# Norm 1's scale and shift moved to ScalarE on transposed rows, modulation sums in column groups, GpSimd in source order, attention's list shifted

## The chip, the cores and the metric

One core of a Trainium2 chip runs the whole kernel. The metric is the device time of one execution in microseconds (us). PE is TensorE's matrix multiply and PEld its weight load, DVE is VectorE, ACT is ScalarE, POOL is GpSimd, and SP is SyncE, which here only issues transfers.

## The reference, cut to what matters

A transformer block for one sequence of 2048 rows and 576 channels. Six modulation vectors come from a condition vector. The first layer norm is scaled and shifted by two of them and feeds a sliding-window attention with 32 heads of 18 channels; the second half (a shifted token mixer and an MLP with 4608 hidden channels) is not touched by the change.

```python
mod = (silu(c) @ w_mod).reshape(1, 6, 1, 576)
sa, ca, ga, sb, cb, gb = mod[:, 0], ..., mod[:, 5]
h = layernorm(x) * (1 + ca) + sa                 # norm 1
q, k, v = split(h @ wqkv)                        # 3 x 32 heads x 18
p = softmax(where(0 <= i - j < 256, q k^T * 18**-0.5, -1e9))
x = x + ga * ((p v) @ wo)
h = layernorm(x) * (1 + cb) + sb
x = x + gb * B(h)                                # mixer and MLP
```

## The kernel before

Matrices are split into a rounded part and the rest of it (F32R), so that one product is the sum of three: high times high, high times low, low times high. The work of attention is in `phase_a`. It makes a list of timed steps (`ev`) and plays it in order of time; the times are in units of 12.5 us, only order the steps, and are no measurement. PE runs its instructions in that order (`manual_schedule` names PE). The other engines' streams, and SP's transfers, are ordered by a scheduler. Each engine works its stream off strictly in order.

**Start.** `cond` loads the condition vector `c` one element to a partition and makes silu of it. `mod_load(v)` loads the part of `w_mod` for vector v (v = 1 is the scale `ca`, v = 0 the shift `sa`) as one tile `wmL`, in one large transfer and one for the last 64 rows. `mod_mm` multiplies a 128-column copy of silu (`silub`) with it, in two halves of 288 columns and five chunks of rows each, so that each sum `pm` stands on all 128 partitions; `mod_ev` evicts it into a row tile `mod`.

**Norm 1** runs for 16 tiles t of 128 rows: `load` (x to a row buffer, tag "r", 5 buffers), `stat` (DVE's bn_stats, POOL's rs), `norm` (`modulate`, L95 to L106: DVE L99 and L101, for t of 2 and more DVE L99 and POOL L103 and L104, on whole rows) and `tr` (`split9`: five PE transposes L68 and L72 into two PSUM tiles `pa` and `pb` of tag "tr" with two buffers, ACT casts L69 and L73 to the high part of `hT`, DVE subtractions L70 and L74 for the low part).

**Projections.** `vproj(t, z)` makes a `pv` (14 matmuls of 288 columns, L316) for half z of the value heads, `qproj(m, g)` a `pq` (14 matmuls of 512 columns, L330) for 128 channels m of queries and keys and 4 tiles g of rows. Order in PE's stream: for g = 0 to 3 four `pv` of z = 0 and the two `pq` of m = 0 and 4, with the transposes of the next group between them; then 16 `pv` of z = 1; then the other `pq`. The weights `Wv` and `Wq` are loaded by SP, cast by ACT and completed by a subtraction on POOL (L280, L294). A `pq` is cast by ACT (L332) and subtracted by DVE (L333) into `hl`, which SP stores to the DRAM tensors `qkh` and `qkl` (L335).

**Attention** works on 32 units of four heads by 512 rows. `ualloc` takes four tiles `U` (three of them in the buffers of `hT`, the fourth in that of `Wq`), and sets them to 0 (DVE, L344) and 1 (POOL, L345). `uload` fills a `U` with 12 loads from `qkh` and `qkl` (SP, L359). `s2` makes the scores `sc` of 16 blocks (PE L385) whose maxima DVE reduces (L392), turns the maxima (`mT`, L406) and writes them into U by a DMA (`ms`, L410); `s3` makes the exponents (`X` on PE L435 and L436, `P` on ACT L442) and the products with V (`av`, L457, four heads on four groups of 32 partitions). The list of attention begins at `shift = t_end + u0`, where `t_end` is the time behind the last `pq`.

The other four modulation vectors are summed up on POOL in `modvec` (chunks L187 to L190), and PE adds over the partitions (L197) at fixed places in attention.

Of the kernel before, what the change touches and what calls it, by code (L numbers as in the profile page):

```python
# [50 lines left out]
class Kern:  # L51
# [75 lines left out]
    def phase_a(self):  # L127
# [10 lines left out]
        with ExitStack() as st:  # L138
# [25 lines left out]
            def cond():  # L164
                ct = sm.tile([P, KC + 1], F32, name="ct", bufs=1)
                nc.vector.memset(ct, 0.0)
                with nc.allow_non_contiguous_dma("condition vector to partitions"):
                    nc.sync.dma_start(ct[:, 0:KC], self.c[0, 0:KC * P].rearrange("(k p) -> p k", p=P))
                    nc.sync.dma_start(ct[:TAIL, KC:KC + 1], self.c[0, KC * P:].rearrange("(k p) -> p k", p=TAIL))
                nc.scalar.activation(silu, ct, AF.Exp, scale=-1.0)  # L170
                nc.vector.tensor_scalar(silu, silu, 1.0, None, op0=ALU.add)
                nc.vector.reciprocal(silu, silu)
                nc.vector.tensor_tensor(out=silu, in0=silu, in1=ct, op=ALU.mult)
# [49 lines left out]

            def mod_bc():
                fm["s"] = pp.tile([P, KC + 1, P], F32, tag="P", name="silub", bufs=self.b_p)
                nc.vector.tensor_copy(fm["s"], silu.unsqueeze(2).to_broadcast([P, KC + 1, P]))

            def mod_mm(v, hf):
                def f():
                    cs = slice(hf * 288, (hf + 1) * 288)  # L230
                    pm = self.ps.tile([P, 288], F32, tag="sc", name=f"pm{v}{hf}", bufs=self.b_sc)
                    for k in range(KC + 1):
                        kk = P if k < KC else TAIL
                        nc.tensor.matmul(pm, fm["s"][:kk, k, :], fm[v][:kk, k, cs], start=(k == 0), stop=(k == KC))
# [3 lines left out]
            def mod_ev(v, hf):
                def f():
                    cs = slice(hf * 288, (hf + 1) * 288)  # L240
                    if hf == 0:
                        mod2[v] = rp.tile([P, D], F32, tag="cs", name=f"mod{v}", bufs=4)
                    nc.scalar.activation(mod2[v][:, cs], fm[v, hf], AF.Copy, bias=1.0 if v == 1 else 0.0)
                return f
# [24 lines left out]

            def vload(z, k):  # L270
                def f():
                    raw = rp.tile([P, 288], F32, tag="wraw", name=f"rwv{z}_{k}", bufs=2)
# [6 lines left out]
                    nc.scalar.copy(w[:, 0, :], raw)
                    nc.gpsimd.tensor_tensor(out=w[:, 1, :], in0=raw, in1=w[:, 0, :].bitcast(F32), op=ALU.subtract)  # L280
# [40 lines left out]
            def qproj(m, g):  # L321
                def f():
# [11 lines left out]
                    for n, dst in enumerate((qkh, qkl)):  # L334
                        nc.sync.dma_start(dst[m * P:(m + 1) * P, g * 512:(g + 1) * 512], hl[:, n, :].bitcast(F32))  # L335
                return f

            def ualloc(n):
                def f():
# [4 lines left out]
                    nc.vector.memset(q.bitcast(F32), 0.0)  # L344
# [728 lines left out]
```

## Time and profile before

| | us |
|---|---|
| median of 3 runs | 1852.71 (1848.93 to 1860.01) |
| profiled execution | 1854.05 |
| its span in the trace | 1851.9 |
| PE busy | 1770.5 (96%) |
| DVE, ACT, POOL busy | 1005.2, 583.4, 399.9 |
| granted TensorE clock, mean | 0.979 of full |

The span runs from the first to the last instruction. A busy PE is no PE at its peak: under a lower granted clock the same matmul is busy for longer, so the clock column is read beside the busy one. In a timeline, the first number is the start, the second the busy time, and brackets hold the idle time of the engine ahead of the group and what ended it.

### The profile page before, as it was taken

To read this page: it belongs to the slowest core of one execution; us is meant where nothing else is said; L and a number is where in the kernel's file an instruction comes from. 1 tells how busy PE (TensorE), PEld (TensorE's weight loads), DVE (VectorE), ACT (ScalarE), POOL (GpSimd) and SP (SyncE) were. 2 spreads that over 40 slices of the span, in tenths; PEclk is the share of its full clock that TensorE was granted. 3 is DMA by queue.
4 is the path that set the end of the run, shared out by engine and by line. 5 is a ranking of instruction groups with operands and counts; after the bars stand their busy time and mean duration, and the time that the engine had idled before them with its cause. 6 is when DMAs were issued, how large, how long until landed. Compare 5 with 4: busy or idle time off the path is not lost.

```text
span 1851.9 us, 30277 instructions
## 1 busy us (share of the span) xinstructions
PE 1770.5 (96%) x11696; PEld 1517.7 (82%) x11696; DVE 1005.2 (54%) x2683; ACT 583.4 (32%) x1212; POOL 399.9 (22%) x389
## 2 busy tenths in 40 slices
PE   6889979999998988899999999999999999999999
PEld 4788856667675776899989999999999999999998
DVE  5601267777775787887744444444444344444433
ACT  2222226656565444434321112111211121112111
POOL 7771100000002011111133323332232111111100
PEclk8999979999998999999999999999999999999999
DMA  6454443333334455642211111111110000000002
GB/s 183 118 145 138 168 129 90 91 96 96 94 97 127 146 181 181 224 154 84 85 53 53 53 34 47 53 53 41 34 47 20 28 28 28 28 28 28 1 1 103
DMA packets 98502, 156.88 MB, mean 85 GB/s; under 512 B 11828, under 2 KB 41268, under 8 KB 98360
## 3 DMA queue, kind: packets, MB, share of 16 engines
q1 hardware_dynamic: 98360, 154.97, 27.3%
q8 instruction: 92, 1.51, 0.3%
q14 instruction: 50, 0.41, 0.1%
HBM read 107.06 MB, written 47.20 MB: 83 GB/s over the span
## 4 chain that ended last, share of the span: by engine, by line
PE 55%; DVE 2%; POOL 1%; issue 0%; ACT 0%; DVEq 0%; ACTq 0%; POOLq 0%
PE p L1001 25%; PE p L972 21%; PE pg L813 2%; PE w L866 2%; PE p L974 2%; PE p L973 2%; DVE x L867 0%; DVE xr L99 0%; PE po L638 0%; DVE G L831 0%; POOL CW L956 0%; DVE LNT L70 0%; DVE G L818 0%; DVE CW L951 0%; DVE xm L740 0%
## 5 line engine op out<-in xcount | busy, mean ns | idle before, releaser
L1001 PEld LDWEIGHTS p<-CW,Gc 128*128 128x128 f32 x3456 | 474.7, 188 | 16.2 <-DVE Gc L983 3.6
L1001 PE MATMUL p<-CW,Gc 128*128 128x288 f32 x3456 | 483.1, 295 | 3.4 <-DVE Gc L983 3.4
L972 PE MATMUL p<-LNT,CW 128*128 128x512 f32 x1728 | 419.3, 391 | 0.0
L972 PEld LDWEIGHTS p<-LNT,CW 128*128 128x128 f32 x1728 | 316.6, 188 | 58.8
L1005 DVE TENSOR_TENSOR acc<-p,acc 128x288 f32<-128x288 f32 x340 | 153.6, 455 | 317.0 <-PE p L1001 313.6
L392 DVE CUSTOM_DVE_ANT_0 sc<-sc,mask 128x384 f32<-128x384 f32 (+2 forms) x512 | 264.4, 553 | 105.8 <-PE sc L385 99.7
L980 ACT ACTIVATE gfc<-p 128x512 f32<-128x512 f32 x144 | 86.2, 599 | 735.7 <-PE p L974 735.7
L442 ACT ACTIVATE P<-X 128x384 f32<-128x384 f32 x480 | 228.7, 490 | 151.7 <-PE X L436 144.7
L385 PE MATMUL sc<-U 126*128 126x384 f32 (+2 forms) x512 | 204.6, 420 | 14.2 <-DMA U<-qkh 7.5
L435 PE MATMUL X<-U 128*128 128x384 f32 (+2 forms) x704 | 194.3, 331 | 10.6 <-ACT P L442 6.8
L435 PEld LDWEIGHTS X<-U 128*128 128x128 f32 x704 | 124.8, 194 | 61.8 <-ACT P L442 31.5
L1005 DVE TENSOR_TENSOR accw<-p,accw 128x288 f32<-128x288 f32 x204 | 90.0, 453 | 130.4 <-PE p L1001 129.1
L436 PE MATMUL X<-maskb,identb 128*128 128x256 bf16 x480 | 138.1, 288 | 0.0
L983 DVE TENSOR_TENSOR Gc<-gfc,Gc 128x512 fp32r<-128x512 f32 x144 | 129.0, 896 | 5.3 <-ACT Gc L982 0.7
L385 PEld LDWEIGHTS sc<-U 126*128 126x128 f32 x512 | 103.1, 207 | 22.3 <-issue 9.0
L330 PE MATMUL pq<-hT,Wq 128*128 128x512 f32 x504 | 120.3, 399 | 0.0
L330 PEld LDWEIGHTS pq<-hT,Wq 128*128 128x128 f32 x504 | 95.2, 190 | 22.4
L952 POOL TENSOR_TENSOR CW<-r,CW 128x1024 fp32r<-128x1024 f32 x17 | 41.2, 2426 | 281.6 <-DVE CW L950 281.6
L457 PE MATMUL av<-P,V 128*32 128x256 f32 (+2 forms) x1472 | 95.0, 392 | 0.0
L982 ACT CAST Gc<-gfc 128x512 fp32r<-128x512 f32 x144 | 89.4, 621 | 4.6
L956 POOL TENSOR_TENSOR CW<-r,CW 128x1152 fp32r<-128x1152 f32 x17 | 46.5, 2733 | 158.4 <-DVE CW L955 158.4
L517 POOL TENSOR_TENSOR wor<-wor,ga 128x576 f32<-128x576 f32 x5 | 7.0, 1401 | 337.5 <-DMA wor<-in_A_wo_dram 337.5
(1076 smaller groups left out, 2027.3 us busy)
## 6 DMA issues: line engine op xcount, KB each, us to landing
U<-qkh SPq DMA_DIRECT2D x160, 72.0 KB
U<-qkh SPq DMA_DIRECT2D x96, 108.0 KB
r<-in_B_w_dram SPq DMA_DIRECT2D x18, 576.0 KB
qkh<-hl SPq DMA_DIRECT2D x36, 256.0 KB
qkl<-hl SPq DMA_DIRECT2D x36, 256.0 KB
r<-in_B_w_dram SPq DMA_DIRECT2D x18, 512.0 KB
U<-qkl SPq DMA_DIRECT2D x80, 72.0 KB
U<-qkl SPq DMA_DIRECT2D x48, 108.0 KB
```

Source lines behind the costliest of these rows:

```text
L330: nc.tensor.matmul(pq, a, b, start=(n == 0), stop=(n == len(pl) - 1))
L385: nc.tensor.matmul(sc[:, lo:], QZ[:KR, q, i * P:(i + 1) * P], KZ[:KR, j, i * P + lo:(i + 3) * P], start=True, stop=True)
L392: nc.vector.tensor_tensor_reduce(out=sc[:, lo:], in0=sc[:, lo:], in1=mask[:, lo:], scale=1.0, scalar=-3e38, op0=ALU.add, op1=ALU.max, accu ...
L435: nc.tensor.matmul(X[:, x0:x0 + nb, :].rearrange("p a b -> p (a b)"), KZ[:, j, kb * P:(kb + 1) * P], QZ[:, q, qb * P:(qb + nb) * P], start ...
L436: nc.tensor.matmul(X[:, 0::2, :], self.identb, mk, start=False, stop=True)
L442: nc.scalar.activation(Pb[b][:, q, :], Xb[b, q].rearrange("p a b -> p (a b)"), AF.Exp, scale=SCALE)
L457: nc.tensor.matmul(abox[0][32 * q:32 * q + 32, q0:q0 + w], V[4 * g + kb][:, hv:hv + 32], Pb[b][:, q, p0:p0 + w], start=(first and n == 0), ...
L972: nc.tensor.matmul(pg, W3[:, ws, fs], L[:, xs, :], start=(i == 0), stop=False)
L982: nc.scalar.copy(Gh, gf)
L983: nc.vector.tensor_tensor(out=Gl, in0=gf, in1=Gh.bitcast(F32), op=ALU.subtract)
L1001: nc.tensor.matmul(po, a, w, start=(i == 0), stop=(i == len(seq) - 1))
L1005: nc.vector.tensor_tensor(out=acc[t][:, cs], in0=po, in1=acc[t][:, cs], op=ALU.add)
```

## The change

- `cond` loads `c` as five rows, and PE turns it onto the partitions (`pc`).
- `mod_load` and `mod_mm` go by row chunks k: two loads of 128 rows, then four matmuls with only 32 columns of silu, one for each quarter q (shift or scale, columns 0 to 255 or 256 to 575), that write four groups of 32 partitions of one PSUM tile `pm`. `mod_ev` evicts the four, and `mod_tr` turns them so that scale and shift stand per channel on partitions (`modT`).
- `norm` is only subtract and multiply on DVE (one `tensor_scalar`). Scale and shift are applied behind the transposes by ACT, five ACTIVATE Identity of 128 columns whose scale and bias are columns of `modT`: four write back into the row tile x, one into PSUM. ACT then casts; the low part of 4 x 128 columns is subtracted by POOL instead of DVE.
- `Wv` is loaded by one large transfer a half (`vraw`); for z = 0 DVE subtracts instead of POOL. The four `pq` of m = 5 stand ahead of the 16 `pv` of z = 1, and the last three m (7, 3, 8) go by groups, so that hT0 is last read nine `pq` ahead of the end (six before).
- The `hl` stores are issued by ACT instead of SP. The `U` zeros are set by POOL instead of DVE.
- POOL runs in the order of the list too; `u0` goes from 0.3 to -1.55, `u_ld` from 0.45 to 0.5, and the times of the start are a new table.

```diff
 def mod_mm(k):
+    for q in range(4):
+        v, cs = q // 2, halves[q % 2]
+        nc.tensor.matmul(fm["p"][32 * q:32 * q + 32, 0:cs.stop - cs.start], fm["s"][:kk, k, :], fm[v][:kk, k, cs], start=(k == 0), stop=(k == KC))
...
 def norm():
-    self.modulate(x, x, box[0], box[1], mod2[1], mod2[0], self.m_eng[t])
+    nc.vector.tensor_scalar(x, x, box[0], box[1], op0=ALU.subtract, op1=ALU.mult)
 def tr():
...
+    for k in range(KC):
+        nc.scalar.activation(h[:, k, :], pa[:, k, :], AF.Identity, bias=mod_col(0, k, r), scale=mod_col(1, k, r))
+    nc.scalar.activation(pb, pb, AF.Identity, bias=mod_col(0, KC, r), scale=mod_col(1, KC, r))
+    nc.scalar.copy(L[:, 0:KC, cs], h)
+    nc.scalar.copy(L[:TAIL, 2 * KC, cs], pb)
+    nc.gpsimd.tensor_tensor(out=L[:, KC:2 * KC, cs], in0=h, in1=L[:, 0:KC, cs].bitcast(F32), op=ALU.subtract)
+    nc.vector.tensor_tensor(out=L[TAIL:, 2 * KC, cs], in0=pb, in1=L[:TAIL, 2 * KC, cs].bitcast(F32), op=ALU.subtract)
...
-    nc.gpsimd.tensor_tensor(out=w[:, 1, :], in0=raw, in1=w[:, 0, :].bitcast(F32), op=ALU.subtract)
+    (nc.gpsimd if z else nc.vector).tensor_tensor(out=w[:, 1, :], in0=raw, in1=w[:, 0, :].bitcast(F32), op=ALU.subtract)
...
-    nc.sync.dma_start(dst[m * P:(m + 1) * P, g * 512:(g + 1) * 512], hl[:, n, :].bitcast(F32))
+    nc.scalar.dma_start(dst[m * P:(m + 1) * P, g * 512:(g + 1) * 512], hl[:, n, :].bitcast(F32))
...
-    nc.vector.memset(q.bitcast(F32), 0.0)
+    nc.gpsimd.memset(q.bitcast(F32), 0.0)
...
-    u0, u_ld = 0.3, 0.45
+    u0, u_ld = -1.55, 0.5
-    with self.tc.manual_schedule(engines={mybir.EngineType.PE}):
+    with self.tc.manual_schedule(engines={mybir.EngineType.PE, mybir.EngineType.Pool}):
```

PE's stream at the start before, from the modulation sums to the first row tile (`x_249` is tile 0):

```order
L234 MATMUL pm_219<-wmL_211,silub 128x288 x5
L234 MATMUL pm_225<-wmL_211,silub 128x288 x5
L234 MATMUL pm_233<-wmL_214,silub 128x288 x5
L234 MATMUL pm_240<-wmL_214,silub 128x288 x5
L68 MATMUL hT0pa<-ident,x_249 128x128 x4
L72 MATMUL hT0pb<-ident,x_249 64x128
```

The same place now; the last of the five chunks and the turns behind it (`pc_320` becomes `modT`):

```order
L242 MATMUL pm<-wmL_255,modx 32x256
L242 MATMUL pm<-wmL_255,modx 32x320
L242 MATMUL pm<-wmL_253,modx 32x256
L242 MATMUL pm<-wmL_253,modx 32x320
L254 MATMUL pc_320<-ident,modx 128x128 x2
L255 MATMUL pc_320<-ident,modx 64x128
L285 MATMUL hT0pa<-ident,x_215 128x128 x4
L287 MATMUL hT0pb<-ident,x_215 64x128
```

The sums moved from 20 matmuls on 128 partitions to 20 on 32 partitions each, three transposes came in behind them, and tile 0's transposes no longer read rows that hold scale and shift.

POOL's stream before, around the subtractions for `Wv` of z = 1 (`Wv_1` to `Wv_3` of that half; `wm` are chunks of `modvec`):

```order
L189 TENSOR_SCALAR wm_3_3986<-wm_3_3986,silu 128x576
L190 TENSOR_TENSOR wm_0_3767<-wm_0_3767,wm_3_3986 128x576
L280 TENSOR_TENSOR Wv_1_1128<-rwv_1_1127,Wv_1_1128 128x288
L280 TENSOR_TENSOR Wv_2_1133<-rwv_2_1132,Wv_2_1133 128x288
L189 TENSOR_SCALAR wm_4_4065<-wm_4_4065,silu 64x576
L190 TENSOR_TENSOR wm_0_3767<-wm_0_3767,wm_4_4065 64x576
L187 TENSOR_SCALAR wm_0_4244<-wm_0_4244,silu 128x576
L189 TENSOR_SCALAR wm_1_4315<-wm_1_4315,silu 128x576
L190 TENSOR_TENSOR wm_0_4244<-wm_0_4244,wm_1_4315 128x576
L280 TENSOR_TENSOR Wv_3_1138<-rwv_3_1137,Wv_3_1138 128x288
```

And now, from the last tile's subtraction on (`x_793` is tile 15):

```order
L296 TENSOR_TENSOR hT_942<-x_793,hT_942 128x4x128
L334 TENSOR_TENSOR Wq<-rwq_1126,Wq 128x640
L320 TENSOR_TENSOR Wv_0_1148<-rwv_1073,Wv_0_1148 128x288
L320 TENSOR_TENSOR Wv_1_1151<-rwv_1073,Wv_1_1151 128x288
L320 TENSOR_TENSOR Wv_2_1154<-rwv_1073,Wv_2_1154 128x288
L320 TENSOR_TENSOR Wv_3_1157<-rwv_1073,Wv_3_1157 128x288
L320 TENSOR_TENSOR Wv_4_1160<-rwt_1075,Wv_4_1160 128x288
L334 TENSOR_TENSOR Wq<-rwq_1475,Wq 128x640
```

The chunks of `modvec` are gone from between them; they now stand behind the eight settings of `U`.

PE's stream before, from the last `pq` to attention:

```order
L330 MATMUL pq_2_1929<-hT_706,Wq 128x512 x14
L330 MATMUL pq_2_1952<-hT_706,Wq 128x512 x14
L330 MATMUL pq_3_1972<-hT_903,Wq 128x512 x14
L330 MATMUL pq_3_1995<-hT_903,Wq 128x512 x14
L385 MATMUL sc_0_0_0_0_2031<-U_1906 128x128
L385 MATMUL sc_0_0_0_1_2033<-U_1906 128x128
L385 MATMUL sc_0_0_0_2_2036<-U_1906 128x128
L385 MATMUL sc_0_0_0_3_2039<-U_1906 128x128
```

And now, from the last `pq` that reads hT0 (`hT_363`) on:

```order
L370 MATMUL pq_0_1855<-hT_363,Wq 128x512 x14
L370 MATMUL pq_1_1875<-hT_514,Wq 128x512 x14
L370 MATMUL pq_1_1898<-hT_514,Wq 128x512 x14
L370 MATMUL pq_1_1930<-hT_514,Wq 128x512 x14
L370 MATMUL pq_2_1950<-hT_733,Wq 128x512 x14
L425 MATMUL sc_0_0_0_0_1974<-U_1895 128x128
L425 MATMUL sc_0_0_0_1_1976<-U_1895 128x128
L425 MATMUL sc_0_0_0_2_1979<-U_1895 128x128
L425 MATMUL sc_0_0_0_3_1982<-U_1895 128x128
L425 MATMUL sc_0_0_1_0_1985<-U_1895 128x256
L370 MATMUL pq_2_1988<-hT_733,Wq 128x512 x14
L425 MATMUL sc_0_0_1_1_2008<-U_1895 128x256
```

The first 25 scores moved in ahead of, among and behind the last five `pq`: five, then four behind each `pq`. From the first `X` on PE's stream is the same as before.

More of the change, by code (lines that the diff above doesn't have):

```diff
@@ L164, in cond @@
             def cond():
[L165 to L173, printed above, removed]
+                fm["x"] = pp.tile([P, 12 * P], F32, tag="P", name="modx", bufs=self.b_p)
+                cr = fm["x"][0:KC + 1, 9 * P:10 * P]
+                sr = fm["x"][0:KC + 1, 10 * P:11 * P]
+                nc.vector.memset(cr, 0.0)
+                nc.sync.dma_start(cr[0:KC, :], self.c[0:1, 0:KC * P].rearrange("o (k p) -> (o k) p", p=P))
+                nc.sync.dma_start(cr[KC:KC + 1, 0:TAIL], self.c[0:1, KC * P:])
+                nc.scalar.activation(sr, cr, AF.Exp, scale=-1.0)
+                nc.vector.tensor_scalar(sr, sr, 1.0, None, op0=ALU.add)
+                nc.vector.reciprocal(sr, sr)
+                nc.vector.tensor_tensor(out=sr, in0=sr, in1=cr, op=ALU.mult)
+                pc = self.ps.tile([P, KC + 1], F32, tag="tr", name="pc", bufs=self.b_tr)
+                nc.tensor.transpose(pc, sr, self.ident[0:KC + 1, 0:KC + 1])
+                nc.vector.tensor_copy(silu, pc)
             def modvec(v):
@@ L238, in mod_ev @@
[L238 to L244, printed above, removed]
+                fm["s"] = fm["x"][:, 4 * P:4 * P + 32 * (KC + 1)].rearrange("p (k n) -> p k n", n=32)
+                nc.vector.memset(fm["x"][:, 256:320], 0.0)
@@ new lines, in mod_ev, with mod_tr @@
+            def mod_ev():
+                fm["r"] = fm["x"][:, 0:320]
+                for q in range(4):
+                    n = halves[q % 2].stop - halves[q % 2].start
+                    nc.scalar.activation(fm["r"][32 * q:32 * q + 32, 0:n], fm["p"][32 * q:32 * q + 32, 0:n], AF.Copy, bias=float(q // 2))
+            def mod_tr():
+                pc = self.ps.tile([P, 3, P], F32, tag="tr", name="pc2", bufs=self.b_tr)
+                for j in range(2):
+                    nc.tensor.transpose(pc[:, j, :], fm["r"][:, j * P:(j + 1) * P], self.ident)
+                nc.tensor.transpose(pc[:TAIL, 2, :], fm["r"][:, 2 * P:2 * P + TAIL], self.ident)
+                v4 = pc.rearrange("p j (q n) -> p q j n", n=32)
+                nc.vector.tensor_copy(modT[:, :, 0:2], v4[:, :, 0:2, 0])
+                nc.vector.tensor_copy(modT[:TAIL, :, 2:3], v4[:TAIL, :, 2:3, 0])
@@ L246, in ln, with mod_col @@
+            def mod_col(v, k, rows):
+                q, j = (2 * v, k) if k < 2 else (2 * v + 1, k - 2)
+                return modT[rows, q, j:j + 1]
             def ln(t):
@@ L565, in phase_a @@
                 else:
-                    first.setdefault(("q", a), T)
                     ev.append((T, qproj(a, b)))
```

101 lines of the change are left out of this document (55 added, 46 removed).

## The prediction

> **What bounds the kernel now.** I read the page's busy shares first, then a table of stages, then who PE waited for, then PE's own order of events.
>
> ```profile
> PE 1770.5 (96%) x11696; PEld 1517.7 (82%) x11696; DVE 1005.2 (54%) x2683; ACT 583.4 (32%) x1212; POOL 399.9 (22%) x389
> ```
>
> PE is the bound, and PE's stream is fixed. So the change can save PE's idle time, and the time that PE runs at a low clock; the rest stays. Where these lie the table of stages shows (start and end, length, then busy us and instructions of PE, PEld, DVE, ACT, POOL, then granted clock, DMA share, GB/s):
>
> ```profile
> 0.00:25.54 25.54, 16.91 (x57) 8.92 (x57) 11.98 (x29) 5.43 (x12) 15.40 (x64) 1.00 0.70 214
> 25.54:36.01 10.47, 4.90 (x20) 3.57 (x21) 7.35 (x11) 4.18 (x10) 10.47 (x9) 0.50 0.30 81
> 36.01:58.55 22.54, 19.50 (x106) 17.30 (x105) 15.80 (x31) 5.42 (x14) 18.53 (x23) 0.86 0.49 145
> 58.55:76.41 17.86, 16.32 (x108) 14.72 (x105) 12.47 (x25) 5.54 (x15) 13.26 (x16) 1.00 0.45 125
> 76.41:94.34 17.93, 16.39 (x107) 14.79 (x105) 6.85 (x15) 5.53 (x15) 11.49 (x14) 1.00 0.44 127
> 94.34:108.47 14.13, 14.13 (x88) 12.86 (x86) 1.57 (x3) 3.40 (x9) 12.61 (x13) 1.00 0.60 165
> 108.47:147.67 39.20, 32.66 (x225) 31.86 (x224) 1.88 (x6) 9.29 (x23) 23.58 (x23) 0.91 0.42 119
> 147.67:239.36 91.69, 91.69 (x394) 73.57 (x392) 23.54 (x30) 18.77 (x32) 12.60 (x9) 1.00 0.47 167
> 239.36:259.06 19.70, 10.93 (x30) 7.18 (x30) 13.12 (x54) 1.16 (x2) 1.38 (x1) 0.61 0.37 110
> 259.06:265.16 6.10, 6.10 (x38) 5.09 (x38) 4.18 (x15) 2.46 (x5) 0.00 (x0) 0.56 0.52 161
> 300.00:900.00 600.00, 565.68 (x4650) 447.78 (x4650) 455.23 (x1546) 318.87 (x730) 52.08 (x97) 0.98 0.42 127
> 900.00:1851.90 951.90, 943.06 (x5640) 858.83 (x5637) 426.39 (x831) 184.29 (x310) 228.48 (x126) 1.00 0.13 40
> ```
>
> The stages are: modulation sums; first transposes; the four groups of `pv` and `pq`; the `pv` of z = 1; the other `pq`; the scores ahead of the first X; attention's first pieces. From 265 on nothing in PE's order changes. What PE waited for in the first 300 us (engine, line, releaser: total, times, longest):
>
> ```profile
> PE sc L385 <- DMA U<-qkh: 6.5, 1, 6.5
> PE pv L316 <- POOL Wv L280: 5.2, 2, 3.3
> PE hT0pa L68 <- DVE x L101: 3.9, 1, 3.9
> PE hT3pa L68 <- POOL Wv L280: 3.0, 1, 3.0
> PE hT6pa L68 <- POOL x L103: 2.9, 1, 2.9
> ```
>
> Each wait stands where the change reaches. PE's events (start, busy, group, idle before):
>
> ```profile
> 10.26 11.34 PE L234 MATMUL pm<-wmL,silub 128*128 128x288 f32 x40 [3.71 <-DVE silub L226]
> 25.54 1.12 PE L68 MATMUL hT0pa<-ident,x 128*128 128x128 f32 x4 [3.94 <-DVE x L101]
> 36.01 7.18 PE L316 MATMUL pv<-Wv,hT 128*128 128x288 f32 x42
> 94.34 7.75 PE L316 MATMUL pv<-Wv,hT 128*128 128x288 f32 x56
> 101.93 6.70 PE L330 MATMUL pq<-hT,Wq 128*128 128x512 f32 x28
> 247.19 7.93 PE L385 MATMUL sc<-U 126*128 126x128 f32 x18 [0.85 <-DMA U<-qkl]
> 264.37 0.86 PE L457 MATMUL av<-P,V 128*32 128x256 f32 x16
> 265.78 0.60 PE L385 MATMUL sc<-U 126*128 126x384 f32 x2
> ```
>
> By starts, a `pv` takes (101.93 - 94.34) / 4 = 1.90 us and a `pq` (108.47 - 101.93) / 2 = 3.27 at full clock. Useful work begins at 36.0.
>
> **A. The start: first `pv` from 36.0 to about 25.7, gain 10.3.** Transfers come first (a window of the queue's full load; the first row tile; the condition vector, whose landing lets ACT's table load begin):
>
> ```profile
> 2.00:16.00 14.00, 10.29 (x36) 5.13 (x34) 4.83 (x17) 2.34 (x5) 4.70 (x42) 1.00 1.00 324
> 12.75 0.46 DVE L85 BATCH_NORM_STATS2 a0st<-x 128x6 f32<-128x288 f32 x1 [2.55 <-DMA x<-in_A_x_dram]
> 7.21 1.28 ACT L170 ACT_TABLE_LOAD   x1 [7.21 <-DMA ct<-in_c_dram]
> ```
>
> The first row tile lands at 12.7 behind 2.95 MB (both `wmL` and itself), that is 9.1 us at 324 GB/s from 2.0 on, and 1.6 more. Now two row tiles, `c` and the ten chunks are first, 3.24 MB: the last chunk lands at 2.0 + 10.0 + 1.6 = 13.6, and `Wv` (0.74 MB) at 15.9. `c` no longer stands behind a large transfer; silu is ready by 8, hidden by the chunks. The sums: before, a record of 288 columns takes 11.34 / 40 = 0.283 us, two records a matmul. In `av`, eight matmuls on four groups of 32 partitions (16 records, 256 and 128 columns) would take 3.0 us at that rate and take 0.8, so the four groups run beside each other. The four of the last chunk then take about 0.6. Evictions, turns and copies follow; ACT's prices come from these rows:
>
> ```profile
> 26.69 0.59 ACT L69 CAST hT<-hT0pa 128x512 fp32r<-128x512 f32 x1 [0.48 <-PE hT0pa L68]
> 27.17 0.43 ACT L279 CAST Wv<-rwv 128x288 fp32r<-128x288 f32 x1
> 27.50 0.26 ACT L73 CAST hT<-hT0pb 64x128 fp32r<-64x128 f32 x1
> 27.66 0.43 ACT L279 CAST Wv<-rwv 128x288 fp32r<-128x288 f32 x1
> ```
>
> POOL's price for a row operation on two tensors (mean 1453 ns for 576 columns), and SP's for issuing a store of `hl`:
>
> ```profile
> L104 POOL TENSOR_TENSOR x<-x,mod 128x576 f32<-128x576 f32 x14 | 20.3, 1453 | 0.8
> 207.34 0.32 SPq L335 DMA_DIRECT2D qkh<-hl  x1
> ```
>
> On ACT, from start to start, 512 columns take 0.48, 288 take 0.33, 128 take 0.16. Four evictions 1.3, three transposes 0.9 (the row of 25.54 has four in 1.12), two small DVE copies 0.4, handing over 0.3: `modT` at 17.1. On ACT five casts of `Wv` stand ahead of tile 0, from 15.9 to 17.6. The new ACTIVATE with scale and bias from partitions is in no row: between 0.16 and 0.48, and I take 0.33, since columns of `modT` have to be fetched. Tile 0 frees its PSUM tile at 17.6 + 4 x 0.33 = 18.9. Since `tr` has two buffers, each next tile costs transposes 1.1 (low clock, as in the second stage), 1.3 on ACT and 0.2 of handing over, 2.6 in all; tile 3's transposes end at 18.9 + 2 x 2.6 + 1.1 + 0.4 = 25.6. POOL's subtraction of a tile (512 of L104's 576 columns, 1.3) lies beside it. Ends: 36.0 - 23 = 13 with 0.16 an ACTIVATE; 4 with 0.48 and sums that run one behind another (20 x 0.57 from 8 on, 19.4 instead of 14.2).
>
> ScalarE: Activation LUTs, What ACT_TABLE_LOAD costs, in the Trainium skill, gives an ACTIVATE 186 ns and 0.833 ns a column, 93 ns more for each operand that is a column of partitions, and an overlap of 93 ns. The 288-column row fits (0.43). For the new ones it gives 0.39 a start; the first `pv` would then come at about 26.5, and ACT would have 15.5 us of work in a group instead of 14.3.
>
> **B. The groups: gain 4.7.** Without its idle 1.54 a group takes 16.3 (the row of 58.55). The first took 22.5, with a low clock at its head and 2.9 of waiting for x rows on POOL. That wait goes: POOL leaves whole-row work for one subtraction, and x loads no longer stand behind `hl` stores on SP. Late next is ACT: four tiles at 5 x 0.33 + 0.48 + 0.16 = 2.3, four V copies at 0.33, two `pq` with a cast 0.59, two stores at 0.32 and 0.7 of waiting for DVE, in all 14.3 of 16.3. The store that waits for DVE holds up the ACTIVATEs behind it, and PE waits for those. So I leave 1 us a group for it: 19.0 for the first (1.6 of low clock), 17.3 for the two others: 3.5 + 0.6 + 0.6. Ends 0 and 7.
>
> **C. The `pv` of z = 1: gain 8.8.** 39.2 against 16 x 1.90 = 30.4. The weights were late since POOL had `modvec` chunks between them and SP loaded row by row. Now four `pq` (13.1 us) stand ahead, beside the two before: 19.6 us for five casts and five subtractions. Ends 7 and 9.
>
> **D. Into attention: gain 7.9.** The rows for issuing four loads of a U and for setting it:
>
> ```profile
> 242.64 1.46 SPq L359 DMA_DIRECT2D U<-qkh  x4
> 219.82 1.38 POOL L345 MEMSET U<- 128x1536 f32 x1 [17.44 <-PE pq L330]
> 226.79 1.76 DVE L344 MEMSET U<- 128x2048 f32 x1 [2.41 <-DMA qkl<-hl]
> ```
>
> Before, the last five `pq` and the stage behind them take 5 x 3.27 + 19.7 = 36.05. Now the 25 scores lie among the `pq`. On PE they cost 0.26 at most (265.78, two of them in 0.52), 6.0 with `mT`. DVE's 13.1 of the stage before lies beside 28 us. Scores share three PSUM buffers with `pq`, and DVE takes a score in about 0.5, so four in a row stall by some 0.6, five times, 3.0. The first U: set by POOL in 1.8 + 1.4 (DVE's time for the zeros, 1.76, taken for POOL's), 12 loads at 0.37, 2.7 to land (last issue 244.5, scores at 247.2): 10.6, against 4 x 3.27 = 13.1 until it is read. But SP's and ACT's transfers share their completion semaphores in turn, and the last two loads take those of the stores of the third `pq` behind hT0: 9.8 + 1.3 for cast and subtraction + 2 to land + 2.7 = 15.8, so 2.7 of waiting. Sum 16.35 + 6.0 + 3.0 + 2.7 = 28.1. Ends: 13.5 without stalls; 0 when loads or buffers cost 8 more.
>
> **E. Clock: gain 2.7.** Behind the wait for U the clock is 0.56 for 6.1 us; at full clock the same takes 3.4. With PE busy through the hand-over it stays up. Ends 0 and 3.5. TensorE: Matmul & The Clock Gate, What's actually happening, in the Trainium skill says that the clock falls to half behind an idle window of about 3.4 us; the trace agrees, with 0.56 behind 6.5 of idling, and by it waits of 2.7 would not bring it down.
>
> **At nothing.** The stores' issues on ACT behind the groups: a `pq` gives ACT 2.0 of 3.27. `modvec`, some 38 us of POOL, moves into attention, where POOL is idle; the PE additions that need it stand over 12 us behind its last chunk. If that cover went, PE would wait there.
>
> The sum is 10.3 + 4.7 + 8.8 + 7.9 + 2.7 = 34.4, from the profiled execution's own 1854.05 (span 1851.9, 2.1 around it): 1819.7. That execution is 1.3 above the median, well inside the runs' spread; I say 1820.
>
> **Rivals.** *ACT limits the groups* (0.17): PE's waits there eat B and half of A. For it: 14.3 of 16.3 us. Against: ACT was busy only 5.5 in a group, and V copies can lag. A = 5, B = 0, rest as above: 24.4, time 1830. The price of ScalarE: Activation LUTs in the Trainium skill (above) speaks for this rival. *The hand-over gains nothing* (0.10): U loads come 8 us late, and the clock falls again, D = E = 0; for it, the 6.5 us of waiting in the old order; 1830. *Slower* (0.04): a tile in ACT's stream, with in-order waits for PE, DVE and POOL's subtractions in source order, costs PE more than the 1.0 it now gains: 16 tiles must each hold PE for 2.2 us more than I assume to eat 34.4; at 3 us more the time is 1868. For it, POOL now cannot step around a late operand; against it, that late work (Wv, x rows) has left POOL. *No change* (0.06): the start stays bound by transfers and the z = 1 wait and hand-over return as other waits: 1850.
>
> **How the numbers follow.** The forecast has 0.63: 1806 to 1833 by its ends not all at once (gain 21 to 48). The two rivals at 1830 lie inside; low of 1806 and high of 1838 leave out the last two, and some of the tails. What a measurement can tell from no change is about 0.5%, 9 us. Faster 0.90, same 0.06, slower 0.04.
>
> **What would show it.** A: the first `pv` near 25.7, `pm` records beside each other, tiles 2.6 apart. B: groups of 17 us, PE's idle time there ended by ACT. C: the 16 `pv` in 30.4 with no wait for POOL. D: first X 28 us behind the start of the last five `pq`, PE never idle over 3 us. E: clock 1.00 there. The forecast is wrong if `pv` of tile 4 to 15 wait for POOL or ACT, or if the second U waits for stores.

## The result, and the profile after

The changed kernel took 1839.3 us (median of 10 runs, 1836.5 to 1845.5), the kernel before 1852.8: a ratio of 0.9922, 95% interval 0.9905 to 0.9939, a gain of 14. The forecast was 1820, with a range of 1806 to 1838. The profiled execution has a span of 1837.0 against 1851.9, and PE's busy time fell by 8.9 us, to the row:

```profile
PE 1761.6 (96%) x11700; PEld 1508.9 (82%) x11700; DVE 984.2 (54%) x2670; ACT 611.1 (33%) x1292; POOL 385.6 (21%) x376
```

The table of stages of the changed kernel, in the columns of the prediction's: sums; first tiles; the groups; fourth group with the four `pq` behind it; `pv` of z = 1; other `pq`; hand-over to the first X; then five stretches of attention and the wo stage.

```profile
0.00:19.29 19.29, 10.27 (x60) 3.62 (x61) 5.45 (x18) 3.92 (x9) 5.93 (x51) 0.88 0.92 268
19.29:30.26 10.97, 5.27 (x21) 3.32 (x21) 9.03 (x25) 10.19 (x29) 6.26 (x9) 0.50 0.43 132
30.26:51.52 21.26, 18.99 (x105) 16.90 (x106) 10.42 (x23) 13.45 (x35) 10.02 (x12) 0.89 0.46 131
51.52:69.59 18.07, 16.60 (x106) 14.77 (x106) 8.87 (x22) 12.27 (x34) 8.16 (x13) 1.00 0.40 124
69.59:86.82 17.23, 16.64 (x106) 14.81 (x106) 5.77 (x13) 12.47 (x35) 8.34 (x13) 1.00 0.44 130
86.82:114.12 27.30, 27.30 (x141) 23.46 (x142) 4.43 (x7) 10.14 (x25) 10.58 (x10) 1.00 0.55 174
114.12:144.20 30.08, 30.08 (x226) 30.07 (x224) 1.19 (x5) 7.21 (x17) 1.56 (x1) 1.00 0.10 29
206.52:237.65 31.13, 25.83 (x101) 19.36 (x99) 13.13 (x54) 4.09 (x7) 4.45 (x4) 0.89 0.39 133
345.00:400.00 55.00, 50.87 (x406) 34.16 (x405) 39.31 (x144) 29.52 (x62) 10.05 (x10) 0.94 0.49 120
540.00:603.32 63.32, 54.63 (x428) 36.47 (x427) 39.06 (x151) 36.05 (x76) 13.93 (x10) 0.92 0.47 134
603.32:900.00 296.68, 273.99 (x2181) 250.37 (x2181) 238.14 (x718) 129.53 (x332) 40.81 (x91) 0.98 0.48 153
```

The same work of the last three rows in the kernel before:

```profile
367.00:417.00 50.00, 47.24 (x407) 32.23 (x406) 38.95 (x144) 29.62 (x63) 0.00 (x0) 1.00 0.35 100
556.00:617.93 61.93, 55.30 (x436) 37.55 (x435) 39.44 (x153) 36.35 (x77) 13.80 (x10) 0.92 0.48 136
617.93:914.60 296.67, 273.67 (x2180) 250.09 (x2180) 237.90 (x717) 129.44 (x332) 40.91 (x91) 0.98 0.48 153
```

Read as a running account, the gain is 5.75 at the first `pv` (36.01 against 30.26), 7.5 at the fourth group, 16.5 ahead of the last five `pq`, 21.4 at the first X (259.06 against 237.65) and 22.3 at 286. Then it is lost again: 5.0 in one stretch of 55 us, where POOL is now busy and was not, some 1 between 400 and 540, 1.4 up to 603. From there on the two agree within 0.4, and 14.9 are left. So two questions stand: why the first 300 us gave 22 and not 34, and what attention lost.

### The profile page after: what moved, and what is told of

Read it like the earlier page. It is cut to its first block, busy times and chain, and to the rows that moved or that the text cites. A ratio compares the mean times of both kernels' runs of the same rounds, so it can differ in the third digit from the quotient of the medians.

```text
span 1837.0 us, 30267 instructions
## 1 busy us (share of the span) xinstructions
PE 1761.6 (96%) x11700; PEld 1508.9 (82%) x11700; DVE 984.2 (54%) x2670; ACT 611.1 (33%) x1292; POOL 385.6 (21%) x376
## 4 chain that ended last, share of the span: by engine, by line
PE 55%; DVE 2%; POOL 1%; issue 0%; DMA 0%; ACT 0%; SPq 0%; DVEq 0%; ACTq 0%; POOLq 0%
PE p L1039 25%; PE p L1010 21%; PE pg L851 2%; PE w L904 2%; PE p L1012 2%; PE p L1011 2%; DVE x L905 0%; DVE xr L99 0%; PE po L676 0%; DMA r<-in_B_w_dram 0%; DVE G L869 0%; POOL CW L994 0%; DVE xm L778 0%; DVE G L856 0%; DVE LNT L70 0%
## 5 line engine op out<-in xcount | busy, mean ns | idle before, releaser
L1018 ACT ACTIVATE gfc<-p 128x512 f32<-128x512 f32 x144 | 86.1, 598 | 735.7 <-PE p L1012 735.7
L476 PEld LDWEIGHTS <-identb 128*128 128x128 bf16 x480 | 46.4, 97 | 35.0 <-issue 14.6
```

The source lines that it names most:

```text
L476: nc.tensor.matmul(X[:, 0::2, :], self.identb, mk, start=False, stop=True)
```

## The experiments

In this table, turns are the time between the 9th and the 14th turn of maxima (`mT`), five units of attention, in the profiled execution; groups are the first three.

| kernel | median, us | ratio to before | first `pv` | groups, sum | first X | turns |
|---|---|---|---|---|---|---|
| before | 1852.8 | | 36.01 | 58.3 | 259.06 | 65.1 |
| changed | 1839.3 | 0.9922 | 30.26 | 56.6 | 237.65 | 70.2 |
| c1 (once more) | 1847.9, one run | | 29.78 | 56.9 | 236.02 | 74.5 |
| e1 PE alone in order | 1848.6 | 0.9966 | 32.05 | 63.2 | 253.31 | 64.4 |
| e2 chunks and additions early | 1841.2 | 0.9924 | 30.60 | 56.3 | 245.17 | 62.9 |
| e3 stores on SP | 1836.0 | 0.9899 | 29.91 | 54.6 | 235.12 | 67.4 |
| e4 no shift | 1838.0 | 0.9902 | 29.61 | 56.0 | 235.02 | 69.1 |
| e5 chunks early | 1841.3 | 0.9935 | 29.97 | 55.9 | 243.28 | 66.6 |
| e6 tail in SBUF | 1828.7 | 0.9885 | 27.73 | 53.5 | 230.54 | 68.7 |
| e7 `Wv` casts on DVE | 1838.5 | 0.9917 | 31.87 | 55.8 | 241.00 | 66.2 |
| e8 e4 + e5 + e6 | 1827.7 | 0.9858 | 28.38 | 54.2 | 235.78 | 65.7 |
| e9 no chunk loads | 1833.1 | 0.9892 | 28.97 | 56.1 | 233.09 | 64.1 |
| e10 e6, u0 -1.25 | 1829.3 | 0.9871 | 28.05 | 53.6 | 229.85 | 74.2 |
| e11 e10, u_ld 1.0 | 1837.2 | 0.9894 | 28.83 | 54.3 | 235.71 | 68.2 |
| e12 e10, chunks late | 1826.8 | 0.9860 | 28.15 | 54.2 | 230.67 | 63.7 |
| e13 e10, chunks first | 1827.0 | 0.9860 | 28.18 | 54.3 | 230.68 | 63.9 |
| e14 e12, stores on SP | 1826.1 | 0.9860 | 28.06 | 49.5 | 232.01 | 65.5 |
| e15 e13, groups' stores on SP | 1824.6 | 0.9852 | 27.23 | 50.7 | 226.31 | 66.0 |
| e16 e12, groups' stores on SP | 1825.3 | 0.9857 | 27.54 | 50.3 | 226.06 | 63.8 |

Intervals of the ratios are 0.0015 to 0.003 to either side; a profiled execution is one of the runs and can lie some us from the median (that of e15 took 1830.5, the longest of its five). Each ratio is to the kernel before as it ran in the same session, with medians of 1852.0 to 1854.8, so between sessions the ratios compare kernels, and not the medians.

Up to the first X, changed, c1 and e9 run the same code. Still their first `pv` comes at 30.26, 29.78 and 28.97, and their first X at 237.65, 236.02 and 233.09. So a difference of 1 or 2 us between single profiles shows no effect there.

### What attention lost: the loads of modvec's chunks

Theory 1: the chunk loads of `w_mod`, which SP issues between the loads of U since `modvec` moved into attention, make U late. Rival 2: PE merely comes at another phase of its loads. First the kernel once more, with no edit.

> The changed kernel once more, nothing edited, to see what of attention's loss comes back in another execution. If the waits for U at 359 to 392 us (3.9 in all) and the dips of the clock behind them (2.8) belong to the order of the transfers, both return within 0.5, and from the 50th to the 650th X it takes 390 to 393. If they are chance of one execution, waits of the same sizes stand elsewhere or the clock stays up, and it is under 388.

Its events of PE (start, busy, group, idle before), below those of the changed kernel's first execution:

```profile
359.66 0.41 PE L425 MATMUL sc<-U 126*128 126x384 f32 x1 [0.74 <-DVE mr L439]
361.50 0.41 PE L425 MATMUL sc<-U 126*128 126x384 f32 x1 [1.43 <-DMA U<-qkl]
376.22 0.43 PE L425 MATMUL sc<-U 126*128 126x384 f32 x1 [0.95 <-DMA U<-qkl]
```

```profile
359.87 0.66 PE L425 MATMUL sc<-U 126*128 126x384 f32 x1 [1.86 <-DMA U<-qkh]
376.41 0.41 PE L425 MATMUL sc<-U 126*128 126x384 f32 x1 [1.29 <-issue]
378.43 0.66 PE L425 MATMUL sc<-U 126*128 126x384 f32 x1 [1.60 <-DMA U<-qkl]
```

The waits come back at the same two places, so these belong to the order; their sizes are chance, and here they were larger (74.5 instead of 70.2). Neither of the two expectations had that, and 1847.9 lies above all ten times of the changed kernel.

The next kernel starts attention at the same phase, without the loads:

> The changed kernel without the 15 transfers of w_mod for the modulation vectors 3 to 5 (a memset by POOL fills each chunk instead, so these three vectors are wrong); nothing ahead of 320 us is changed, so attention starts at the same phase. Theory 1 (chunk loads among U loads): PE's waits for U between 345 and 400 us fall from 3.9 to under 2.4, the clock stays up there, and from the 50th to the 650th X it takes 386 to 388 instead of 392: time 1834 to 1836. Rival 2 (phase of the U loads and of the clock's gate): waits and dips stay, 390 to 392 and 1838 to 1841.

```diff
+if v == 2:
     nc.sync.dma_start(w[:kk], self.w_mod[...])
+else:
+    nc.gpsimd.memset(w[:kk], 0.01)
```

The five units of the changed kernel and then of this one (columns as above):

```profile
338.37:408.60 70.23, 65.92 (x531) 44.84 (x530) 50.19 (x185) 38.98 (x83) 12.29 (x13) 0.95 0.50 127
```

```profile
334.44:398.51 64.07, 62.14 (x530) 42.84 (x530) 49.55 (x185) 39.00 (x83) 0.00 (x0) 1.00 0.38 103
```

The turns take 6.2 less and the clock stays at 1.00: theory 1 holds. Not all of the median's gain is the edit's, since in its profile the first X, which stands ahead of the edit, came 4.6 sooner. The edit also took the chunks' arithmetic on POOL out of this stretch (12.29 us to 0.00); but it is U that PE waits for, and SP's stream shows why U is late. The last loads of one U in the changed kernel, whose twelve began at 351.64:

```profile
355.07 0.32 SPq L399 DMA_DIRECT2D U<-qkl  x1
356.05 0.85 SPq L188 DMA_DIRECT2D wm<-in_w_mod_dram  x2
357.59 0.29 SPq L399 DMA_DIRECT2D U<-qkl  x1
358.32 0.29 SPq L399 DMA_DIRECT2D U<-qkh  x1
```

And in e9, where they began at 347.73:

```profile
349.69 1.42 SPq L402 DMA_DIRECT2D U<-qkh  x4
351.15 0.70 SPq L402 DMA_DIRECT2D U<-qkl  x2
352.06 0.27 SPq L402 DMA_DIRECT2D U<-qkh  x1
```

Two chunk loads stand ahead of U's last two, and from the first to the last of the twelve it takes 6.7 us instead of 4.3. The three other kernels move the loads instead of leaving them out.

> The changed kernel, but only PE is held to the order of the list; POOL is scheduled freely again, as before, so that the modvec chunks and their 20 loads come between 60 and 180 us instead of 16 of them in attention. Theory 1 (the chunks' loads on SP, between the loads of U, made attention lose about 6 of the 22 us that were won up to 290): attention from 286 to 665 takes 372 to 374 us as before instead of 379, PE's waits for U there fall from 4.6 to about 3; but chunks stand between Wv subtractions again, which may cost up to 3 ahead of 110. In all 1833 to 1838. Rival 2 (U is late because PE comes at another phase of its loads, whatever POOL does): attention as in the changed kernel, 379, in all 1838 to 1842.

```diff
-with self.tc.manual_schedule(engines={mybir.EngineType.PE, mybir.EngineType.Pool}):
+with self.tc.manual_schedule(engines={mybir.EngineType.PE}):
```

> The changed kernel with POOL in the order of the list, but with the modvec steps written into the list between the first pv of z = 1 and the settings of U (about 115 to 175 us) and their PE additions 6 us behind each. Theory 1: no chunk load is left in attention, so the 379 us from the mT at 286 to the end of the wo stage become 373 or so, the dips of the clock at 361 and 376 go, and nothing is paid for it ahead: 1832 to 1835. Rival 2: still 379, 1838 to 1841. A third way: chunks delay the Wq subtractions or the settings of U, and the hand-over is longer by over 3.

```diff
-ev += spread(mv[:-1], shift + 8.0 + 2.5 * n, shift + 10.0 + 2.5 * n)
-ev.append((shift + 11.3 + 2.5 * n, mv[-1]))
+a, b = first["v", 1] + 0.1, self.t_end - 9.5 * dq
+a, b = a + (b - a) * n / 4, a + (b - a) * (n + 1) / 4
+ev += spread(mv[:-1], a, b)
+ev.append((b + 0.5, mv[-1]))
```

> The changed kernel with only the modvec chunks moved ahead (115 to 175 us), the four additions on PE left at their places in attention, so that the sums keep four of the five row buffers and the weights of the output projection cannot come early as they did in the kernel with the additions moved too (there three casts of them stood ahead of the first P on ACT for 9.8 us). Theory 1, chunk loads among U loads: from the 50th to the 650th X it takes 380 to 383 us instead of 392.0, the hand-over stays as in the changed kernel (first X 237 to 238), in all 1828 to 1831. Rival 2, phase of the loads: 389 to 392 and 1838 to 1841. Rival 3, the 379 to 382 of the two kernels without chunks there came from their late start of attention: between, 385 to 388.

The edit of e5 is that of e2 without its last line: the additions stay where they were. In all three the turns shorten (64.4, 62.9, 66.6), and in all three the time does not fall, since the first X comes 5.6 to 15.7 later. In e1 the groups took 63.2, and PE waited 1.40 and 4.68 for POOL's subtraction of `hT` in the fourth. In e2, PE waited 2.15 and 2.02 for DVE's `hl` ahead of the first X, where the additions now stand, too. Behind the first X, the row buffers were free early, so the casts of the output weights, which wait for POOL, came to stand ahead of the first P on ACT, and X waited:

```profile
255.45 0.67 ACT L558 CAST Wom<-wor 128x576 fp32r<-128x576 f32 x1 [2.86 <-POOL wor L557]
```

```profile
256.57 0.69 PE L475 MATMUL X<-U 128*128 128x256 f32 x2 [9.78 <-ACT P L482]
```

In e5 it is POOL's order itself. Its stream: the chunks wait behind a `Wq` subtraction and for their single free row buffer, and the setting of the first U behind the last of them; then PE's wait for that U:

```profile
186.06 1.58 POOL L334 TENSOR_TENSOR Wq<-rwq,Wq 128x640 fp32r<-128x640 f32 x1 [9.29 <-ACT Wq L333]
198.98 0.75 POOL L194 TENSOR_SCALAR wm<-wm,silu 64x576 f32<-64x576 f32 x1 [3.25 <-DMA wm<-in_w_mod_dram]
201.18 1.81 POOL L384 MEMSET U<- 128x2048 f32 x1
```

```profile
214.43 0.44 PE L425 MATMUL sc<-U 126*128 126x128 f32 x1 [6.08 <-DMA U<-qkh]
```

Two more runs put the loads elsewhere in attention, on top of e10 (below):

> The kernel with the tail in SBUF and u0 -1.25, with the chunk loads and additions of vectors 3 to 5 moved 4.5 units (some 56 us) later in attention. If the place counts (behind 400 us U has slack, in the changed kernel no clock was lost from 420 to 540 with five loads there): no dip between 340 and 420, where 5.7 were lost with u0 -1.25, from the 50th to the 650th X 385 to 388 instead of 392.7, in all 1822 to 1825. If any 15 loads among U loads cost the same, the dips move behind 400 and the time stays at 1828 to 1831.

> The same kernel with the chunk loads of vectors 3 to 5 moved ahead instead, to 250 to 345 us, where no kernel so far has waited over 0.7 for U. If U has slack there: no dip from 340 to 420, 385 to 388 from the 50th to the 650th X, 1822 to 1826. If the loads make waits wherever they stand: waits for U of 1 to 2 us between 250 and 345, and 1828 to 1833.

```diff
+d = 4.5 if n else 0.0                    # e12
+ev += spread(mv[:-1], shift + d + 8.0 + 2.5 * n, shift + d + 10.0 + 2.5 * n)
+ev.append((shift + d + 11.3 + 2.5 * n, mv[-1]))
...
+ev += spread(mv[:-1], shift + 1.0 + 2.0 * n, shift + 3.0 + 2.0 * n)    # e13
```

Their medians are 2.3 to 2.5 below e10's, by the ratios it is 2.0, inside the intervals; 4 to 7 were expected. The turns fell to 63.7 and 63.9, but the waits moved with the loads; in e12:

```profile
458.06 0.41 PE L426 MATMUL sc<-U 126*128 126x384 f32 x1 [1.65 <-DMA wm<-in_w_mod_dram]
459.83 0.66 PE L426 MATMUL sc<-U 126*128 126x384 f32 x1 [1.36 <-DMA U<-qkl]
```

A score reads no `wm`: the profile names the transfer that landed last. SP issued three chunk loads from 454.13 on, and the last load of a U behind them, at 456.55.

Over all profiles the eight with these loads between the 9th and 14th turn (changed, c1, e3, e4, e6, e7, e10, e11) take 66.2 to 74.5, mean 69.8; the eleven without them 62.9 to 66.6, mean 64.7. The loads cost about 5 there. From the first X to the end, these eight take 1601.1 on average, the five with the loads elsewhere in attention 1596.9, and the six with none in attention 1592.9, each with a spread of 8 to 16: about half of the cost comes back wherever in attention the loads stand. SP's order is one way, as the rows above show; what the load on the DMA engines (0.50 instead of 0.38) adds was not separated.

### The start and the groups: the tail in PSUM, and the stores on ACT

> The changed kernel with the scaled tail of a tile (pb) written to a tile in SBUF instead of back into PSUM, so that its tr buffer is free behind the ACTIVATE and not behind cast and DVE's subtraction. If the start and the groups are set by that buffer (PE waited 1.07 + 1.49 + 1.66 there for DVE L297 up to 30 us and 4.3 in the groups): first pv at 27 to 28.5 instead of 30.3, groups 0.5 to 1 shorter each, in all 1834 to 1837. Rival: ACT itself is the limit of the tiles (2.7 us of work each), the waits turn into waits for ACT: first pv at 29.5 to 30.3 and 1838 to 1841.

```diff
-nc.scalar.activation(pb, pb, AF.Identity, bias=..., scale=...)
+pt = rp.tile([P, D], F32, tag="cs", name=f"hT{t}pt", bufs=4)[:TAIL, 0:P]
+nc.scalar.activation(pt, pb, AF.Identity, bias=..., scale=...)
```

PE's events at tiles 2 and 3 in the changed kernel, and in e6:

```profile
24.65 1.11 PE L285 MATMUL hT2pa<-ident,x 128*128 128x128 f32 x4
27.25 0.42 PE L287 MATMUL hT2pb<-ident,x 128*64 128x128 f32 x1 [1.49 <-DVE hT L297]
30.19 0.42 PE L287 MATMUL hT3pb<-ident,x 128*64 128x128 f32 x1 [1.66 <-DVE hT L297]
```

```profile
24.04 1.11 PE L285 MATMUL hT2pa<-ident,x 128*128 128x128 f32 x4 [1.39 <-ACT x L291]
26.75 1.11 PE L285 MATMUL hT3pa<-ident,x 128*128 128x128 f32 x4 [1.39 <-ACT x L291]
```

The waits for DVE are gone, the first `pv` comes 2.5 sooner, and the three groups take:

```profile
27.73:46.97 19.24, 17.51 (x107) 15.84 (x105) 13.08 (x26) 13.87 (x37) 10.87 (x13) 0.94 0.62 186
46.97:64.22 17.25, 16.75 (x108) 14.85 (x105) 9.96 (x21) 12.43 (x35) 9.05 (x12) 1.00 0.44 124
64.22:81.24 17.02, 16.46 (x108) 14.85 (x105) 10.05 (x17) 12.95 (x37) 9.23 (x13) 1.00 0.44 127
```

The median is 10.6 us lower; by the ratios, 0.9885 against 0.9922, it is 7, and 2 to 5 were expected. Not all of it is the edit's: the fourth group began at 81.24 instead of 86.82, 5.6 sooner, but at 82.2 on average of the six profiles with this tail and the stores on ACT (e6, e8, e10 to e13; 81.24 to 83.12), against 86.1 of the six without it (changed, c1, e2, e4, e5, e9; 85.07 to 86.87). That is 3.9, clear of chance. Of e6's start, only 0.6 of the 2.5 lies ahead of the first tile (hT0pa at 18.66 instead of 19.29); the rest is the tail.

> The changed kernel with the five casts of Wv for z = 0 on DVE and their subtractions on POOL, so that tile 0 stands behind nothing on ACT. ACT had 18.57 to 20.39 full of these casts while hT0pa was ready at 20.2 at the latest: if ACT is what delays tile 0, its ACTIVATEs start at 19.9 or so and the first pv comes 0.4 to 0.8 sooner; if the transposes behind modT do (19.29 to 20.35), nothing changes: 0 to 0.3. In all 1836 to 1840 with either.

```diff
-nc.scalar.copy(w[:, 0, :], raw)
+(nc.scalar.copy if z else nc.vector.tensor_copy)(w[:, 0, :], raw)
-(nc.gpsimd if z else nc.vector).tensor_tensor(out=w[:, 1, :], ...)
+nc.gpsimd.tensor_tensor(out=w[:, 1, :], ...)
```

Neither came: the first `pv` was 1.6 later, as PE waited 3.7 for DVE at hT2pb. DVE's stream, behind which the tail's subtraction stands, was the tighter one. The time did not change.

> The changed kernel with the hl stores issued by SP again instead of ACT. By the prediction (a store that waits for DVE on ACT holds up the ACTIVATEs of the next tiles) the three groups between 30 and 87 us become 0.5 to 1 shorter each, and the U loads on SP stand behind the last stores: hand-over 0 to 3 longer; in all 1836 to 1842. The rival, that the groups are set by the two tr buffers alone, gives unchanged groups (21.3, 18.1, 17.2 within 0.2).

```diff
-nc.scalar.dma_start(dst[m * P:(m + 1) * P, ...], ...)
+nc.sync.dma_start(dst[m * P:(m + 1) * P, ...], ...)
```

The groups took 20.45, 17.17 and 16.95, 2.0 less in all, as the prediction's mechanism had it: a store on ACT that waits for DVE. Here it stands in ACT's stream of the changed kernel, between the first and the other ACTIVATEs of tile 6:

```profile
45.88 0.34 ACTq L375 DMA_DIRECT2D qkh<-hl  x1
48.39 0.33 ACTq L375 DMA_DIRECT2D qkl<-hl  x1
48.77 1.15 ACT L291 ACTIVATE x<-hT6pa,modT 128x128 f32<-128x128 f32 x3 [2.55 <-DVE hl L373]
```

The first X came 2.5 sooner: the groups' gain and 0.35 of the start came through the hand-over whole, where up to 3 of loss was expected; c1 and e9 differ as much without an edit. With the tail off PSUM:

> The kernel with the tail in SBUF, u0 -1.25 and the late chunks, with the hl stores issued by SP. In the changed kernel the stores on SP made the groups 2 us shorter. If that came from the store that waits for DVE on ACT, ahead of the next tile's ACTIVATEs, 0.5 to 2 are left with the tail in SBUF: 1 to 2 below the run without; if from the tr buffer, nothing is left, and U loads on SP behind the last stores make the hand-over 0 to 3 longer: the same to 3 above.

The groups took 17.14, 16.15 and 16.16 us, 4.8 less than those of e12, which is the same but for the stores. The hand-over gave that back (29.2 from the first score to the first X, where e12 took 25.4), with PE waiting behind SP's stores:

```profile
202.84 0.30 PE L426 MATMUL sc<-U 126*128 126x128 f32 x1 [2.31 <-DMA qkh<-hl]
```

### The hand-over

> The changed kernel with u0 and u_ld of before (0.3 and 0.45): attention's list not shifted. By the prediction's term D the shift gave most of the hand-over's gain: from the start of the last five pq to the first X 35 to 36 us instead of 31.1, and the first U again waited for over 3 us with a low clock behind it: 1843 to 1848. Rival: the deeper order of the last pq (nine behind hT0 instead of six) alone lets U be loaded in time, and the shift is worth under 2: 1838 to 1841.

```diff
-u0, u_ld = -1.55, 0.5
+u0, u_ld = 0.3, 0.45
```

The rival holds: the time stays, and the first X comes 2.6 sooner, within what c1 and e9 show with the shift. U lands in time without it (the first score, at 221.65, follows on the last `pq`); the shift puts scores in front of PE before U is there. Whether the nine `pq` behind hT0, POOL's setting of the zeros or the stores on ACT let U land in time was not separated. From the start of the last five `pq` to the first X it takes 235.02 - 221.65 + 5 x 3.27 = 29.7; with the shift it is 31.1, and 29.8 and 28.4 in c1 and e9. One `pq` more ahead of the first score:

> The kernel with the tail in SBUF, and attention's list shifted by 0.3 less (u0 -1.25 instead of -1.55), so that one pq more (3.3 us) stands ahead of the first score. By term D the wait for U ahead of the first score was 2.8 and brought the clock down for some 1.5 more: if U has landed when PE comes, no wait over 0.5 and no dip stand there, and the first X comes at 226 to 229 instead of 230.5, in all 1824 to 1828. Rival: the scores behind pile up (fewer pq to lie among), buffers' stalls eat it, first X 230 to 232, 1828 to 1831.

From the first score to the first X, with four `pq` among the scores:

```profile
204.44:229.85 25.41, 20.39 (x86) 14.82 (x85) 13.62 (x57) 3.51 (x6) 7.50 (x6) 0.98 0.44 149
```

With the fifth `pq` that is 28.7. No wait for U stands there, but one of 1.38 for DVE and one of 1.31 for `ms`, and behind the last the clock fell (0.72 in the next 10 us). Of e6's 29.7 only 1 was gained. What was gained is steadiness: e12, e13, e15 and e16, with the same u0, take 28.7 too, where the kernels with -1.55 and nothing else changed there (changed, c1, e9, e6) take 28.4 to 31.1. The turns of e10 took 74.2 beside the chunk loads, and in all it is no faster than e6.

> As the run with u0 -1.25, and u_ld 1.0 instead of 0.5: SP issues a unit's loads ahead of the maxima (ms) and the outputs (od) of the unit before, where it issued them behind. If attention's waits for U (5.6 us from 260 on with the tail in SBUF) come from SP's order, they fall under 3 and the time is 3 to 6 below that of the run with 0.5. Rival: the loads wait for the buffer of the unit four before and not for SP, waits stay within 1 us; or ms behind loads that wait holds up X, which is slower by 3 or more.

The rival, and more: waits for U vanished, and X waited for `ms` instead, 5.58 once and 3.50 at 351; 8 us slower than e10 by the medians (its profile is the longest of its five, 1848.7).

> The changed kernel with three edits together: chunks early with additions left in place, u0 and u_ld of before (no shift), and the tail in SBUF. If the three are independent and theory 1 holds: first X at about 233, the 50th to 650th X in 381 to 384, in all 1823 to 1828. If attention's loss is set by the phase of the loads, 1833 to 1838.

1827.7, inside what independence gave, if with a first X at 235.8 and not at 233: PE waited twice for DVE's `hl` among the `pv` of z = 1, 3.0 in all. The turns took 65.7.

### Put together

> The kernel with the tail in SBUF, u0 -1.25 and the chunk loads first in attention, with the hl stores of m = 0 and 4 (those in the groups) issued by SP and the others by ACT. If the two effects are separate: groups as short as with all stores on SP (first pv to the end of the fourth group 62.5 to 63.5 us), hand-over as without (first X 31 to 32 us behind the first score's... that is at 226 to 227), in all 1821 to 1824. Rival: stores on either queue hold up U through the shared completion semaphores, and the hand-over gives it back: 1825 to 1828.

> The same with the chunk loads late in attention. If the place is worth nothing in itself, it comes out within 2 us of the run with the loads first: 1820 to 1826.

```diff
-nc.scalar.dma_start(dst[m * P:(m + 1) * P, ...], ...)
+(nc.sync if m in early else nc.scalar).dma_start(dst[m * P:(m + 1) * P, ...], ...)
```

The groups keep most of the stores' gain (50.7 and 50.3, where e13 and e12 take 54.3 and 54.2), and the first X comes at 226.3 and 226.1, 4.4 and 4.6 sooner. In all e15 takes 1824.6, ratio 0.9852 (0.9828 to 0.9876), between its two expectations, and e16 1825.3. e15 is faster than the kernel before by 28 and than the changed one by about 13 (1839.3 x 0.9852 / 0.9922 = 1826.3). Of the 4.4 at the first X, the ratios show 1.5 and 0.6 against e13 and e12, inside the intervals.

## Why the prediction was wrong

Faster was right; 1820 was not, and 1839.3 lies above the high of 1838. The terms, by the running account:

| term | predicted | measured | in other runs |
|---|---|---|---|
| A, first `pv` | 10.3 | 5.75 | 8.3 (e6) |
| B, groups | 4.7 | 1.8 | 4.8 (e6), 8.9 (e14) |
| C, `pv` of z = 1 | 8.8 | 9.0 | |
| D, hand-over | 7.9 | 4.9 | 6.3 (c1), 7.6 (e9), same code |
| E, clock | 2.7 | 0.9 | 0.3 (c1), 0.0 (e9), same code |
| at nothing: `modvec` and the rest | 0 | -7.4 | -3.2 (e9) |

**A and B** failed at one step: "Tile 0 frees its PSUM tile at 17.6 + 4 x 0.33". That priced `pa`'s ACTIVATEs and forgot `pb`, whose ACTIVATE writes back into PSUM, so that it is held through two casts and a subtraction in DVE's order. The ACTIVATE's price was right: tile 0's four start at 20.39 and the next at 21.77, 0.345 each against 0.33 taken. So were the groups: with the tail moved they take 19.24, 17.25 and 17.02, forecast 19.0, 17.3 and 17.3; and the 1 us left for the store on ACT is what e14 shows (16.15). The other 2 of A went ahead of the tiles: the last chunk's sums began at 15.56, where 13.6 was taken, and took 1.29 instead of 0.6, and the four evictions took 1.64 instead of 1.3. Why the chunks came late was not tested.

**C** held: PE ran from 86.82 to 144.20 without a wait. Less the 13.1 us of the four `pq` moved in, that is 44.3 against 53.3.

**D** had the right wait, 3.03 us for U against 2.7, and the right reason: SP issued the last two loads of that U at 206.70 and 207.31, after a break of 4.8 us, behind two stores that ACT issued at 204.05 and 204.78. What failed is the step, told under E, that waits of 2.7 us leave the clock up. Behind this one a `pq` was busy for 5.70 us, where the next took 3.54:

```profile
209.77 1.48 PE L425 MATMUL sc<-U 126*128 126x128 f32 x4 [3.03 <-DMA U<-qkl]
211.04 5.70 PE L370 MATMUL pq<-hT,Wq 128*128 128x512 f32 x14
```

The same stretch, from the first score to the first X, in c1 and in e9, beside the row 206.52:237.65 of the changed kernel:

```profile
206.27:236.02 29.75, 24.55 (x100) 18.36 (x99) 13.14 (x54) 4.09 (x7) 4.45 (x4) 0.94 0.41 139
204.66:233.09 28.43, 23.08 (x100) 17.18 (x99) 13.11 (x54) 4.09 (x7) 4.45 (x4) 1.00 0.44 146
```

The code is the same, and PE waits 3.03, 2.93 and 2.89 us for U. The clock is 0.89, 0.94 and 1.00, and the stretch takes 31.1, 29.8 and 28.4, where 28.1 was forecast. So D's sum was right for a clock that stays up. The lower clock cost the changed kernel 2.75 us of busy time against e9 (25.83 instead of 23.08), and which of the three comes is chance. The shift, which D counted on, gave nothing: without it e4 takes 29.7 and e8 28.6.

**E** came where it was worked out: from 237.65 to 244.14 the clock is 1.00, where it was 0.56 behind the first X. Then it was partly lost. From the first X to the fifth turn, before and after:

```profile
259.06:308.03 48.97, 46.25 (x369) 32.33 (x369) 35.00 (x129) 26.55 (x56) 0.00 (x0) 0.91 0.34 100
237.65:285.71 48.06, 44.31 (x370) 30.50 (x369) 36.37 (x134) 26.48 (x56) 11.14 (x11) 0.96 0.39 109
```

PE is busy for 1.9 less and idle for 1.0 more. It waits 1.64 and 1.30 for a later U at 244.55 and 246.27, for which the prediction has no term.

**At nothing** was the costliest miss. `modvec` was costed as 38 us of POOL, where POOL is idle, and its PE additions were indeed never waited for. But 15 of its 20 transfers now also stand on SP among those of U, where PE already waited (1.16 at 382.65 before). Of the 7.4 the run without them gave 4.2 back; the other 3.2, more waits of X for ACT and one of 1.6 for `or` around 600 us among them, were not tested. These are sizes of single executions: c1, the same code, lost 17 there. The rule to count every DMA of a moved step was kept for the stores and not for the chunks.

The two rivals at 1830 came nearer in time than 1820. "The hand-over gains nothing" is not what happened (4.9). "ACT limits the groups" had A and B nearly right, with 5 and 0 against 5.75 and 1.8, but by luck: it was a held PSUM tile and a store that waited, and not ACT's busy time.

## What to carry to other kernels

An operation that writes back into PSUM holds the buffer for everything behind it: count the hold to its last reader, on the engine whose order decides when that one runs. A step moved off a busy place takes its transfers with it; price these against the queue and the buffers that they land among, even if its arithmetic is free. Where work is pulled forward over a boundary, the operand's arrival sets how far: with no shift at all the first X came as soon as with the whole of it.
